# Two more pairs transposed by DMA instead of TensorE, and four output stores held back

## The chip, the cores and the metric

The kernel runs on one core of a Trainium2 chip. The metric is the device time of one execution in microseconds (us), given as the median over runs. Matmuls run on TensorE (PE), their weight loads are listed apart (PEld), and the other engines are VectorE (DVE), ScalarE (ACT), GpSimd (POOL) and SyncE (SP, which here only issues DMAs).

## The reference, cut to what matters

A chunked linear recurrence (4 batches, 8 heads, 768 positions, head size 32, state size 16) gives `x`, 3072 tokens by 256; a gated layer follows:

```python
L = exp(cum[i] - cum[j]) * (i >= j)                 # decay inside a chunk
y = ((C @ B.T) * L) @ x + (C @ state) * exp(cum)    # per batch, head, chunk
state = decay * state + (B * decay_from_j).T @ x
...
gate = maximum(x @ w_gate, 0)                       # 256 -> 1536
out = (gate * (x @ w_val)) @ w_out                  # 1536 -> 256
```

## The kernel before

**Tiling.** The 3072 tokens are cut into 12 pairs of 256 tokens (two chunks of 128) for the recurrence, and into 6 blocks of 512 tokens (two pairs) for the gated layer. While block `b` runs through the layer, the recurrence of the pairs of the next block is threaded between its matmuls: `P = 2b+2` and `Q = 2b+3`, and `W = 2b+1` is finished late. In block 1 these are pairs 4 and 5 (and W = 3), in block 2 pairs 6 and 7 (and W = 5).

**Order.** The order of the instructions on each engine is the order in the program text; `in_order` pins it. So an instruction that waits holds up all that stand behind it on its engine. Loads, stores and DMA transposes share SP's queue in the same way.

**The layer.** For each of 12 slices `f` of the 1536 columns, `gv` (or `gvh` in two halves) makes gate and val on PE, relu on ACT, and the product `h` on DVE; `fout` multiplies `h` by `w_out`; `foevac` copies the result to a buffer `ob` (three buffers that rotate) and stores it through SP.

**The recurrence of a pair.** B and C are loaded raw (`bcr`), and x (`xr`). POOL multiplies B and C by decay factors (`scale...`) and casts x to `xb` (`to_x`). B and C must then be transposed:

- Pairs 0 to 5: POOL writes `bs`; `turn` transposes it on PE (four 128x128 transposes in a pair, `transp`, L393), `bevac` copies B's result to `BT` on ACT, and `cevac` makes two masked copies `CT` of C's.
- Pairs 6 to 11 (`p >= NDMA`): `scale_padded` writes a zero-padded buffer `bz` (three of them, `turned`), with the two masked copies of C already in place, and one DMA transpose (L310) gives `TT`, read by PE directly.

`G` makes C times B transposed (L456; `G_rows`, L495, for pairs 6 on), `gevac` masks it on ACT, DVE and POOL (POOL's part is the affine selects, L171), `Dm` multiplies it with x (L634 and L687), `inter` adds the state's part (L623), `states` and `states_two` make the states (L573, L702), and `yevac` casts the result to `yT`, which the gates of the next block read.

**The stretch of the change.** In block 1 `turn(4)` and `turn(5)` stand among the gates at f = 6 and f = 8. `states(4)` stands at the beginning of the block, `inter(4)` at the end of the gates, `G(4)` and `G(5)` in the output matmuls. `states_two((6, 7))` stands near the beginning of block 2. In blocks 2 to 4 `Dm_two` stands behind eight of the twelve matmuls of the last output tile, and the last four cover the `yT` copies.

Of the kernel before, what the change touches and what calls it, by code (L numbers as in the profile page):

```python
# [8 lines left out]
FP32 = mybir.dt.float32  # L9
# [20 lines left out]
def kernel(  # L30
# [13 lines left out]
    nc = tc.nc  # L44
# [29 lines left out]
    def place(p):  # L74
        b, c0 = p // PPB, 2 * (p % PPB)
        return b, c0, slice(c0 * 128, (c0 + 2) * 128)
# [25 lines left out]
    def load(p, q):  # L102
        if "bcr" not in st.setdefault(p, {}):
            new_bc(p)
        load_bc(p, 1, q)
        load_bc(p, 0, q)
        new_x(p)
        for i in range(2):
            load_x(p, i, q)
# [183 lines left out]
    def scale_padded(p, eng, part=None):  # L293

        b, c0, _ = place(p)
        z = turned[p % 3]
        if part != 1:
            f = fac[:, b, c0:c0 + 2].rearrange("s i j h -> s i (j h)")
            eng.tensor_tensor(  # L299
                out=z.rearrange("s (i k) (h n) -> s i (k h) n", k=4, n=N)[:, :, 0:2 * NH],  # L300
                in0=st[p]["bcr"].rearrange("s i j h n -> s i (j h) n"),
                in1=f.to_broadcast([128, 2, 2 * NH, N]), op=ALU.mult)
            st[p]["B"] = [z[:, 4 * i] for i in range(2)]
        if part == 0:
            return
        parts = z.rearrange("s (i k) (q t n) -> s i k t q n", k=4, q=4, t=2)
        for t in range(2):
            eng.tensor_copy(out=parts[:, :, 2 + t, t], in_=parts[:, :, 1, t])
        tt = st[p]["TT"] = att.tile([128, 8, 128], BF16, tag="TT", name="TT", bufs=4)
        nc.sync.dma_start_transpose(out=tt, in_=z.rearrange("s k n -> s (k n)"))  # L310

    def new_bs(p):
        st[p]["bs"] = att.tile([128, 4, 128], BF16, tag="bs", name="bs", bufs=6)
# [38 lines left out]
    def scale_one(p, eng, j):  # L352

        b, c0, _ = place(p)
        for i in range(2):
            f = fac[:, b, c0 + i, j].rearrange("s (t q) -> s t q", t=2)
            eng.tensor_tensor(
                out=st[p]["bs"][:, 2 * i + j].rearrange("s (q t n) -> s t q n", q=4, t=2),
                in0=st[p]["bcr"][:, i, j].rearrange("s (t q) n -> s t q n", t=2),
                in1=f.to_broadcast([128, 2, 4, N]), op=ALU.mult)  # L360
# [60 lines left out]
    def ct(p, i, rows=slice(0, 128), t=None):  # L421
        if p < NWIDE:
            c = st[p]["CT"][rows, :, :, 64 * i:64 * i + 64]
        else:
            c = st[p]["CT"][rows, :, i]
        return c if t is None else c[:, t]

    def split(p, ap):

        return ap.rearrange("s t (r m) -> s t r m", r=2) if p < NWIDE else ap  # L430
# [17 lines left out]
    def G(p):  # L448
        s = st[p]
        if "gp" not in s:  # L450
            G_banks(p)
        g = s["gp"]
        for i in range(2):
            for q in range(4):
                r = slice(32 * q, 32 * q + 32)
                nc.tensor.matmul(  # L456
                    out=split(p, g[q][:, i]), lhsT=s["BT"][r, i], rhs=ct(p, i, r),
                    start=(i == 0), stop=True, tile_position=(32 * q, 0),
                    skip_group_check=True)
        s["gs"] = att.tile([128, 4, 4, 128], BF16, tag="gs", name="gs", bufs=2)  # L460
# [336 lines left out]
    def fout_last(b):  # L797

        r0 = b * 512 + 384
        for m in range(2):  # L800
# [6 lines left out]
            (nc.vector.tensor_copy if m else nc.scalar.copy)(out=ob, in_=o)  # L807
            (nc.sync if m else nc.scalar).dma_start(out=out[r0:r0 + 128, ms], in_=ob)

    def foevac(b, ts, o=None):  # L810
        last = b == NBLK - 1 and ts == 2
        if ts % 2 == 0 and not last:
            return
        ob = ffn.tile([128, 2, DM], FP32, tag="ob", name="ob", bufs=3)
        r0 = b * 512 + ts * 128
        if last:
            nc.scalar.copy(out=ob[:, 0], in_=fst["o"][:, 0])
            nc.scalar.dma_start(out=out[r0:r0 + 128, :], in_=ob[:, 0])
            return
        nc.scalar.copy(out=ob, in_=o or fst["o"])  # L820
        rows = out[r0 - 128:r0 + 128, :].rearrange("(i p) m -> p i m", p=128)
        for part in ((slice(0, 1), slice(1, 2)) if b in (2, 3) and ts == 3 else (slice(0, 2),)):
            nc.sync.dma_start(out=rows[:, part], in_=ob[:, part])


    B_, C_ = slice(0, 1), slice(1, 2)
# [91 lines left out]
    def turn(p):  # L918
        transp(p, 1)
        transp(p, 0)  # L920

    def tevac(p, beng, *cengs):
        bevac(p, beng)
        cevac(p, *cengs)
# [49 lines left out]
    for b in range(NBLK):  # L974
        P, Q, W = 2 * b + 2, 2 * b + 3, 2 * b + 1
        more = P < NPAIR
        if b == 1:
            load(P + 2, nc.sync)
            load(P + 3, nc.sync)
        if b == 2:  # L980
            scale(Q, nc.gpsimd)
            load(Q + 2, nc.sync)

        nh = (4, 6, 8, 0)[min(b, 3)]
        for f in range(nh):
            if b == 0:
                continue
            turning = f == (3 if b == 1 else nh - 3)
            gvh_mm(b, f, 0)
            gvh_relu(b, f, 0)  # L990
            gvh_mul(b, f, 0)
            if b == 1 and f == 1:
                to_x(P, nc.scalar)
            if turning:
                inter(W, 0)
                inter(W, 1)
                Dm(W)
                if b == 1:
                    states(P)
                    scale_one(P, nc.gpsimd, 1)  # L1000
                else:
                    states_two((P, Q))
                yevac(W, nc.scalar)
                if b == 1:
                    spread(P)
                else:
                    sums_two((P, Q))
# [4 lines left out]
        for f in range(nh, NF):  # L1012
            gv(b, f, b > 2 and f == 0)
            if b == 0:
                if f == 5:
                    over_sum(de_ps)
                if f == 7:
                    sevac(1, 1)
                if f == 9:
                    turn(P)  # L1020
                    tevac(P, nc.scalar, nc.vector)
                if f == 10:
                    held(Q, bc=False)
                if f == 11:
                    back(P)
                    backevac(P, nc.scalar)
            elif b == 1:
                if f == nh:
                    turn(P)
                    tevac(P, nc.scalar, nc.vector)  # L1030
                    scale(Q, nc.gpsimd)
                if f == 8:
                    turn(Q)
                    tevac(Q, nc.scalar, nc.vector)
                    scale(Q + 1, nc.gpsimd)
                    load(Q + 3, nc.sync)
            elif b == 2:
                if f == 9:
                    load(Q + 3, nc.sync)
            elif b == 3:  # L1040
                if f in (2, 6):
                    scale(P + 2 + f // 4, nc.gpsimd)
        if b == 1:
            inter(P, 0)
            inter(P, 1)
        if b == 0:

            for third in range(3):
# [16 lines left out]
                if third == 1:  # L1065
# [11 lines left out]
            A_ps[0] = rest  # L1077
            Dm(P)
            states(Q)
            held(Q + 2)  # L1080
            fout(b, 3, range(4))
            inter(P, 0)
            inter(P, 1)
            gevac(Q, after={2: lambda: [yevac_half(P, t, nc.scalar) for t in range(2)],
                            3: lambda: spread(Q)})
            new_bs(Q + 1)
            scale_one(Q + 1, nc.gpsimd, 0)
            fout(b, 3, range(4, NF))
            foevac(b, 3)
            continue  # L1090
        elif b == 1:
            fout(b, 0)
            G(P)
            gevac(P)
            over_sum2(de)
            fout(b, 1)
            foevac(b, 1)
            fout(b, 2)
        elif more:
            ahead = (P + 2, Q + 2) if Q + 2 < NPAIR else ()  # L1100
            fout(b, 0, range(9), True)
            G_rows(P)
            opened = y_banks()
            inter_rows(P, opened)
            inter_rows(Q, opened)
            gevac(P)
            if b == 2:
                scale_padded(Q + 2, nc.gpsimd, 0)
            fout(b, 0, range(9, NF))
            fout(b, 1)  # L1110
            first_two = fst["o"]
            fout(b, 2, range(1))
            G_rows(Q)
            gevac(Q)
            if b == 2:
                scale_padded(Q + 2, nc.gpsimd, 1)
                load(Q + 4, nc.sync)
                to_x(Q + 2, nc.scalar)
            foevac(b, 1, first_two)
            fout(b, 2, range(1, NF))  # L1120
            fout(b, 3, range(8))
            Dm_two((P, Q))
            states_two(ahead)
            yevac_two((P, Q))
            sums_two(ahead)
            fout(b, 3, range(8, NF))
            foevac(b, 3)
            continue
        else:
            fout(b, 0)  # L1130
            fout(b, 1)
            foevac(b, 1)
            fout(b, 2)
            foevac(b, 2)
            fout_last(b)
            continue
# [40 lines left out]
```

## Time and profile before

| | |
|---|---|
| median of 3 runs | 121.92 us (121.68 to 122.03) |
| profiled execution | 121.89 us, its span 120.2 us, so 1.69 us lie around the span |
| busy share of the span | PE 97%, DVE 73%, ACT 65%, POOL 42% |
| granted TensorE clock | full in every slice |
| DMA moved | 13.70 MB |

The span is cut by the profile in 40 slices of 3 us. A group of matmuls in the chain of waits is shown with the time from its start to that of the next piece, so its pieces add up to the span; the groups' mean of one matmul is its whole duration, which overlaps that of its neighbours.

### The profile page before, as it was taken

The page shows a single profiled execution, that of the slowest core. Times are in us where ns is not written, and L with a number is a line of the kernel's source. Part 1 is how long each engine was busy: PE and PEld are TensorE (multiplying, and loading weights), DVE is VectorE, ACT ScalarE, POOL GpSimd, SP SyncE. Part 2 cuts the span into 40 slices and gives each one's busy share as a digit, 9 for nine tenths or more (in the row PEclk, how much of TensorE's full clock was granted, in tenths as well). Part 3 has the DMA queues.
Part 4 walks back from the last instruction along what each step waited for, and adds up shares of the span by engine and source line. Part 5 has one row for each costly group of instructions (what it writes and reads, how often), then busy time and mean ns, then how long its engine had stood idle before and what let it go on. Part 6 is the DMA issues. An engine that isn't in the chain of part 4 may idle for free.

```text
span 120.2 us, 3322 instructions
## 1 busy us (share of the span) xinstructions
PE 116.1 (97%) x1237; PEld 75.0 (62%) x1237; DVE 87.6 (73%) x206; ACT 77.7 (65%) x170; POOL 50.4 (42%) x102
## 2 busy tenths in 40 slices
PE   7999999999999999999999999999999999999990
PEld 2446754677885577887577544578444677444790
DVE  6896779976899866899775787856787775678500
ACT  4288977687998726888626776535767445767240
POOL 6788999744406271956047542433400033000000
PEclk9999999999999999999999999999999999999999
DMA  3999999999969999799999699922200002200022
GB/s 67 213 187 176 206 185 196 205 128 124 160 69 193 125 100 138 100 172 169 118 171 104 94 145 147 266 68 87 87 0 5 0 0 93 87 0 0 0 87 87
DMA packets 80595, 13.70 MB, mean 114 GB/s; under 512 B 73420, under 2 KB 80580, under 8 KB 80580
## 3 DMA queue, kind: packets, MB, share of 16 engines
q1 hardware_dynamic: 73092, 10.55, 56.3%
q0 software_dynamic: 4080, 2.36, 14.2%
q10 hardware_dynamic: 3408, 0.59, 2.6%
q8 instruction: 9, 0.15, 0.5%
q14 instruction: 6, 0.05, 0.1%
HBM read 11.13 MB, written 3.15 MB: 119 GB/s over the span
## 4 chain that ended last, share of the span: by engine, by line
PE 95%; ACT 1%; DVE 0%; issue 0%
PE o L792 26%; PE gate L747 19%; PE val L747 19%; PE gv L762 14%; PE w L200 4%; PE g L495 2%; PE g L456 2%; PE y L687 1%; PE y L634 1%; PE o L804 1%; PE tp L393 1%; PE A_ps L237 1%; PE y L623 1%; ACT CT L417 1%; PE bt L437 1%; PE y L674 0%
## 5 line engine op out<-in xcount | busy, mean ns | idle before, releaser
L751 DVE TENSOR_TENSOR h<-r,val 128x512 bf16<-128x512 bf16 x54 | 36.9, 687 | 9.1 <-ACT r L750 6.6
L750 ACT ACTIVATE r<-gate 128x512 bf16<-128x512 f32 x54 | 32.2, 597 | 11.9 <-PE gate L747 11.2
L792 PE MATMUL o<-wo,h 128*128 128x256 bf16 x276 | 33.8, 273 | 0.0
L747 PE MATMUL val<-yT,wv 128*128 128x512 bf16 x108 | 32.6, 379 | 0.0
L747 PE MATMUL gate<-yT,wg 128*128 128x512 bf16 x108 | 32.6, 379 | 0.0
L792 PEld LDWEIGHTS <-h 128*128 128x128 bf16 x276 | 25.7, 98 | 5.4 <-issue 1.2
L171 POOL TENSOR_SCALAR_AFFINE_SELECT gs<-gs 128x512 bf16<-128x512 bf16 (+1 forms) x24 | 12.1, 528 | 27.8 <-ACT gs L468 27.8
L479 DVE TENSOR_TENSOR gs<-g,masks 128x512 bf16<-128x512 f32 x24 | 15.4, 685 | 6.0 <-PE g L495 2.8
L747 PEld LDWEIGHTS <-wv 128*128 128x128 bf16 x108 | 10.6, 98 | 12.5
L747 PEld LDWEIGHTS <-wg 128*128 128x128 bf16 x108 | 10.4, 98 | 11.1
L772 DVE TENSOR_TENSOR h<-r,gv 128x256 bf16<-128x256 bf16 x36 | 14.2, 417 | 1.3 <-ACT r L769 1.1
L769 ACT ACTIVATE r<-gv 128x256 bf16<-128x256 f32 x36 | 13.7, 389 | 1.2
L468 ACT CAST gs<-g 128x512 bf16<-128x512 f32 x12 | 7.0, 586 | 11.2 <-PE g L495 5.8
L762 PE MATMUL gv<-yT,wg 128*128 128x256 bf16 x72 | 13.9, 273 | 0.2
L762 PE MATMUL gv<-yT,wv 128*128 128x256 bf16 x72 | 13.9, 273 | 0.0
L299 POOL TENSOR_TENSOR bz<-bcr,fac 128x512 bf16<-128x512 f32 x6 | 6.4, 1059 | 7.1 <-DMA bcr<-in_B_dram 7.1
L820 ACT COPY ob<-o 128x512 f32<-128x512 f32 x11 | 6.5, 591 | 4.2 <-PE o L792 4.1
L322 ACT CAST yT<-y 128x256 bf16<-128x256 f32 (+1 forms) x11 | 5.4, 516 | 4.7 <-PE y L687 2.8
L762 PEld LDWEIGHTS <-wv 128*128 128x128 bf16 x72 | 7.0, 98 | 1.1 <-issue 0.3
L762 PEld LDWEIGHTS <-wg 128*128 128x128 bf16 x72 | 6.8, 98 | 1.0 <-issue 0.2
L200 PE MATMUL w<-const-bfloat16-1.0 128*128 128x512 bf16 (+3 forms) x15 | 5.7, 498 | 0.8 <-PEq L1161 0.8
L322 POOL CAST xb<-xr 128x512 bf16<-128x512 f32 (+1 forms) x8 | 4.7, 591 | 3.2 <-DMA xr<-in_x_dram 3.1
(118 smaller groups left out, 110.8 us busy)
## 6 DMA issues: line engine op xcount, KB each, us to landing
xr<-in_x_dram SPq DMA_DIRECT2D x24, 128.0 KB, 3.2
out_dram<-ob SPq DMA_DIRECT2D x9, 256.0 KB, 2.4
bcr<-in_B_dram SPq DMA_DIRECT2D x16, 64.0 KB, 2.9
bcr<-in_C_dram SPq DMA_DIRECT2D x16, 64.0 KB, 2.9
wg<-in_moe_w_gate_dram POOLq DMA_DIRECT2D x6, 128.0 KB, 4.4
wv<-in_moe_w_val_dram POOLq DMA_DIRECT2D x6, 128.0 KB, 4.9
wo<-in_moe_w_out_dram POOLq DMA_DIRECT2D x3, 256.0 KB, 7.2
out_dram<-ob SPq DMA_DIRECT2D x4, 128.0 KB, 2.5
```

The lines of the kernel that those rows point to most:

```text
L171: nc.gpsimd.affine_select(out=dst, in_=dst, pattern=pattern, compare_op=ALU.is_ge, fill=0.0, base=0, channel_multiplier=-1)
L200: nc.tensor.matmul(out=w[:, 0:cols], lhsT=nc.const_aps.tensor(1.0, [128, 128], BF16), rhs=nc.const_aps.tensor(1.0, [128, cols], BF16), sta ...
L322: (eng.copy if eng is nc.scalar else eng.tensor_copy)(out=out, in_=in_)
L468: nc.scalar.copy(out=d[:, 0], in_=g[0])
L479: nc.vector.tensor_tensor(out=d[:, q], in0=g[q], in1=m, op=ALU.mult)
L747: nc.tensor.matmul(out=o, lhsT=w_tile(ws, f, k), rhs=yT[:, k, tk], start=(k == 0), stop=(k == 1), skip_group_check=True)
L750: nc.scalar.activation(r, g, AF.Relu)
L751: nc.vector.tensor_tensor(out=fst[b][:, f], in0=r, in1=v, op=ALU.mult)
L762: nc.tensor.matmul(out=gv_[:, j], lhsT=w_tile((wgs, wvs)[j], f, k), rhs=yT[:, k, tk], start=(k == 0 and not (early and j)), stop=(k == 1), ...
L769: nc.scalar.activation(r[:, 0:256], fst[b, f, u][:, 0], AF.Relu)
L772: nc.vector.tensor_tensor(out=fst[b][:, f, u * 256:(u + 1) * 256], in0=fst.pop((b, f, u, "r"))[:, 0:256], in1=fst.pop((b, f, u))[:, 1], op ...
L792: nc.tensor.matmul(out=o[:, ts % 2], lhsT=fst[b][:, f, ts * 128:(ts + 1) * 128], rhs=wo[:, f], start=(f == 0 and new), stop=(f == NF - 1), ...
```

## The change

Pairs 4 and 5 go the way of the DMA transposes. A new `scale_turned` writes B and the two masked copies of C into the padded buffer in four POOL instructions per pair; `turn_padded` is the DMA transpose. `G`, `inter` and `states` of these pairs read `TT` and `bz`. `turn`, `bevac` and `cevac` of the two pairs go (eight PE transposes, two ACT copies, four DVE copies). The transposes of pairs 4 and 5, and the loads around them, stand in a new order on SP. `to_x(5)` moves to the beginning of block 1, `to_x(6)` behind `gevac(4)`. The four stores of blocks 0 and 1 get four buffers of their own and are issued behind the gates of block 3; the last stores of blocks 2 and 3 are no longer split in two. In block 4 `Dm_two` stands one output matmul earlier (behind seven).

```diff
+        turn_padded(p)
+
+    def scale_turned(p, eng):
+        b, c0, _ = place(p)
+        z = turned[p % 3]
+        dst = z.rearrange("s (i k) (q t n) -> s i k t q n", k=4, q=4, t=2)
+        src = st[p]["bcr"].rearrange("s i j (t q) n -> s i j t q n", t=2)
+        f = fac[:, b, c0:c0 + 2]
+        for j in range(2):
+            for t in range(2):
+                eng.tensor_tensor(
+                    out=dst[:, :, j * (2 + t), t], in0=src[:, :, j, t],
+                    in1=f[:, :, j, 4 * t:4 * t + 4].to_broadcast([128, 2, 4, N]), op=ALU.mult)
+        st[p]["B"] = [z[:, 4 * i] for i in range(2)]
+
+    def turn_padded(p):
         tt = st[p]["TT"] = att.tile([128, 8, 128], BF16, tag="TT", name="TT", bufs=4)
-        nc.sync.dma_start_transpose(out=tt, in_=z.rearrange("s k n -> s (k n)"))
+        nc.sync.dma_start_transpose(out=tt, in_=turned[p % 3].rearrange("s k n -> s (k n)"))
...
-            c = st[p]["CT"][rows, :, i]
+            c = st[p]["TT"][rows, 4 * i + 2:4 * i + 4]
...
-                    out=split(p, g[q][:, i]), lhsT=s["BT"][r, i], rhs=ct(p, i, r),
+                    out=split(p, g[q][:, i]), rhs=ct(p, i, r),
+                    lhsT=s["BT"][r, i] if p < NWIDE else s["TT"][r, 4 * i],
...
-        ob = ffn.tile([128, 2, DM], FP32, tag="ob", name="ob", bufs=3)
+        early = b < 2
+        ob = ffn.tile([128, 2, DM], FP32, tag="obe" if early else "ob", name="ob",
+                      bufs=4 if early else 3)
...
-        for part in ((slice(0, 1), slice(1, 2)) if b in (2, 3) and ts == 3 else (slice(0, 2),)):
-            nc.sync.dma_start(out=rows[:, part], in_=ob[:, part])
+        if early:
+            late_store.append((rows, ob))
+        else:
+            nc.sync.dma_start(out=rows, in_=ob)
...
         if b == 1:
-            load(P + 2, nc.sync)
+            new_bc(P + 2)
+            load_bc(P + 2, 1, nc.sync)
+            load_bc(P + 2, 0, nc.sync)
+            scale_turned(Q, nc.gpsimd)
+            turn_padded(Q)
+            new_x(P + 2)
+            for i in range(2):
+                load_x(P + 2, i, nc.sync)
             load(P + 3, nc.sync)
+            to_x(Q, nc.gpsimd)
...
                     states(P)
-                    scale_one(P, nc.gpsimd, 1)
...
             elif b == 1:
-                if f == nh:
-                    turn(P)
-                    tevac(P, nc.scalar, nc.vector)
-                    scale(Q, nc.gpsimd)
                 if f == 8:
-                    turn(Q)
-                    tevac(Q, nc.scalar, nc.vector)
-                    scale(Q + 1, nc.gpsimd)
+                    scale_padded(Q + 1, nc.gpsimd)
                     load(Q + 3, nc.sync)
...
+        if b == 3:
+            for rows, ob in late_store:
+                nc.sync.dma_start(out=rows, in_=ob)
...
-            held(Q + 2)
+            held(Q + 2, with_x=False)
...
-            new_bs(Q + 1)
-            scale_one(Q + 1, nc.gpsimd, 0)
+            scale_turned(Q + 1, nc.gpsimd)
+            turn_padded(Q + 1)
+            new_x(Q + 2)
+            for i in range(2):
+                load_x(Q + 2, i, nc.sync)
...
             gevac(P)
+            to_x(P + 2, nc.gpsimd)
             over_sum2(de)
...
-            fout(b, 3, range(8))
+            early = 8 if ahead else 7
+            fout(b, 3, range(early))
...
-            fout(b, 3, range(8, NF))
+            fout(b, 3, range(early, NF))
```

More of the change, by code (lines that the diff above doesn't have):

```diff
@@ L808, in fout_last @@
             (nc.sync if m else nc.scalar).dma_start(out=out[r0:r0 + 128, ms], in_=ob)
+    late_store = []
     def foevac(b, ts, o=None):
```

## The prediction

> **What bounds the kernel now.** I read the page's busy shares first, then its chain by engine, then the stretches around block 1.
>
> ```profile
> PE 116.1 (97%) x1237; PEld 75.0 (62%) x1237; DVE 87.6 (73%) x206; ACT 77.7 (65%) x170; POOL 50.4 (42%) x102
> DMA  3999999999969999799999699922200002200022
> ...
> PE 95%; ACT 1%; DVE 0%; issue 0%
> ```
>
> PE is busy for 97% of the span and carries 95% of the chain that ended last. So time comes off only where PE gets less to do or loses a wait, and time is added only where PE must wait. The DMA engines are nine tenths busy or more in most of the first 26 slices (3 us each, so to 78 us), and much less after that. The chain in order of time shows the stretch of the change (start, length, what).
>
> ```profile
> 36.61 0.43 PE val L747 x2
> 37.04 0.22 PE tp L393 x4
> 37.26 0.43 PE gate L747 x2
> ...
> 38.99 0.22 PE tp L393 x4
> ...
> 41.80 0.22 PE y L623 x4
> ...
> 46.76 0.33 PE g L456 x8
> ...
> 51.68 0.12 PE A_ps L702 x16
> ```
>
> Each piece starts where the last one ends: 36.61 + 0.43 = 37.04, + 0.22 = 37.26. There is no gap in which PE waits, so a step taken out here shortens the chain by its own piece. One microsecond of the same stretch by engine (PE, PEld, DVE, ACT, POOL, clock, DMA share, GB/s) agrees: PE 1.00 at full clock.
>
> ```profile
> 38.00:39.00 1.00, 1.00 (x9) 0.53 (x8) 1.00 (x3) 0.73 (x2) 0.57 (x1) 1.00 1.10 116
> L393 PE MATMUL tp<-ident,bs 128*128 128x128 bf16 x20 | 2.2, 227 | 0.0
> ```
>
> **Part 1: eight PE transposes go.** The chain gives 0.22 us for four, so 2 x 0.22 = 0.44 us come off. The group's mean of 227 ns is one transpose from its beginning to its end; in the chain one starts every 0.22 / 4 = 55 ns, because they overlap, and 55 ns is what I take. The Trainium skill's page "TensorE: Matmul & The Clock Gate", section "Part 4: PE-mode transpose", gives about 275 ns for one 128x128 transpose inside a kernel; by that figure eight would be an estimate of 2.2 us and the sum 119.6 us. The trace shows 227 ns as the duration, near that figure, and 55 ns as the step, and the step decides.
>
> The two ACT copies to BT and the four DVE copies to CT that go with the transposes lie beside PE, which has no gap there; I cost them at nothing. The G and inter matmuls keep their number and shape with other operands: 0.33 and 0.22 us stay.
>
> **Part 2: what PE will wait for instead.** Pair 4's `TT` must have landed for `inter(4)`, at 41.80 - 0.44 = 41.36, pair 5's for `G(5)` at 46.76 - 0.44 = 46.32, pair 4's scaled B for `states(4)`, which now starts at 32.31. POOL first, then SP:
>
> ```profile
> 32.31 0.26 PE L573 MATMUL A_ps<-xb,bs 128*32 128x64 bf16 x12
> 29.88 0.76 POOL L357 TENSOR_TENSOR bs<-bcr,fac 128x128 bf16<-128x128 f32 x2
> 31.56 0.40 POOL L357 TENSOR_TENSOR bs<-bcr,fac 128x128 bf16<-128x128 f32 x1 [0.22 <-DMA bcr<-in_C_dram]
> 36.13 1.20 POOL L348 TENSOR_TENSOR bs<-bcr,fac 128x256 bf16<-128x256 f32 x2 [4.17 <-DMA bcr<-in_B_dram]
> 48.89 1.06 POOL L299 TENSOR_TENSOR bz<-bcr,fac 128x512 bf16<-128x512 f32 x1
> 50.48 0.61 POOL L322 CAST xb<-xr 128x512 bf16<-128x512 f32 x1
> ```
>
> ```profile
> 28.12 1.41 SPq L92 DMA_DIRECT2D bcr<-in_C_dram x2
> 29.62 0.57 SPq L823 DMA_DIRECT2D out_dram<-ob x1
> 31.52 2.67 SPq L92 DMA_DIRECT2D bcr<-in_B_dram x2
> 35.54 0.82 SPq L823 DMA_DIRECT2D out_dram<-ob x1
> 39.23 1.20 SPq L100 DMA_DIRECT2D xr<-in_x_dram x2
> 43.72 1.23 SPq L100 DMA_DIRECT2D xr<-in_x_dram x2
> 45.05 2.88 SPq L310 DMA_TRANSPOSE TT<-bz x1
> L310 SPq DMA_TRANSPOSE TT<-bz x6: 1251/1299/2882, 45.0 to 76.6; - x6
> DMA to landing us min/median/max: 2.7/3.2/5.5
> ```
>
> `states(4)`: the B part of `scale_turned(4)` is again two instructions of 0.40 us; before they ran from 29.88 to 30.64, and nothing ahead of them changes. 1.7 us of room.
>
> Pair 4's transpose: its C part is two more instructions of 0.40 us, from 31.56 on (the last C has landed), so to 32.36. On SP the transpose stands behind pair 5's B, whose issue ended at 31.52 + 2.67 = 34.19; without the store ahead of it that is 0.57 earlier, 33.6, and later than POOL. So: issue 33.6, landing 3.2 after the issue's start at the median, 36.8; at the longest, 5.5, 39.1. Needed at 41.36: 2.3 to 4.6 us of room.
>
> Pair 5's transpose: POOL began pair 5's scaling at 36.13, when its B had landed; now some 0.57 sooner, 35.6, and four instructions of 0.40 end at 37.2. On SP it stands where pair 6's x began, 39.23; both stores are gone (-0.57 - 0.82) and pair 4's transpose is ahead (+1.30): 39.1. Landing 42.3, at the longest 44.6; needed at 46.32: 1.7 to 4.0 us of room.
>
> What is queued behind: everything up to pair 7's x, which ended its issue at 43.72 + 1.23 = 44.95. Now -0.57 - 0.82 + 2 x 1.30 = +1.21, so 46.16. Of two like issues the second starts 0.6 sooner, 45.5.
>
> ```profile
> xr<-in_x_dram SPq DMA_DIRECT2D x24, 128.0 KB, 3.2
> ```
>
> It lands at 45.5 + 3.2 = 48.7. POOL cast pair 7's x at 50.48, now at 50.04 (it hangs on `G(5)` through the affine selects, which come 0.44 sooner); PE wants it in `states_two` at 51.68 - 0.44 = 51.24, and the cast takes 0.61, so PE waits only if it lands after 51.24 - 0.61 = 50.63. Room 1.9 us. Pair 7's B, loaded just before, is needed at 48.45 by the scaling on POOL, with the same slack to PE behind it. I cost the two added DMA transposes and their waits at nothing on PE; the bounds are zero and the case of the second rival, below. Below nothing they cannot go, as PE has no wait here that earlier loads could remove.
>
> `to_x(6)` now stands behind the affine selects of `G(4)`, where POOL next waits for `G(5)`; `to_x(5)` stands ahead of block 1's gates and its reader, `states(5)`, behind them. Both nothing.
>
> **Part 3: the stores.** Two 256 KB stores of block 0 and two of block 1 leave the busy stretch. They come back behind the last transposes:
>
> ```profile
> 75.18 2.65 SPq L310 DMA_TRANSPOSE TT<-bz x2
> 82.36 33.39 SPq L823 DMA_DIRECT2D out_dram<-ob x6
> ```
>
> SP is free from 77.83 to 82.36, 4.5 us; four issues at the 0.82 us above are 3.3 us, and the DMA row above has at most two tenths from there on. Nobody reads these buffers again, and the three other buffers wait only for stores a block older. Nothing on PE, nothing at the end of the kernel, 35 us later.
>
> **Part 4: block 4's `Dm_two` one matmul earlier.**
>
> ```profile
> 100.95 0.58 ACT L322 CAST yT<-y 128x512 bf16<-128x512 f32 x1 [1.12 <-PE y L687]
> 101.12 0.54 PE o L792 x4
> 101.66 0.30 PE gate L747
> 101.96 0.22 PE val L747
> ```
>
> The first gate of block 5 takes 0.30 where the next matmul of that size takes 0.22: its `yT` is cast until 101.53, and 0.08 us of waiting is left. With five output matmuls as cover instead of four (0.54 / 4 or 5: 0.11 us more) it goes. -0.08 us; the other end is nothing.
>
> **Sum.** Profiled execution 121.89 - 0.44 - 0.08 = 121.37 us. That execution lies 0.03 below the median of 121.92, so 121.40 us. The runs before spread from 121.68 to 122.03; about 0.3% (0.37 us) is what a measurement can tell from no change, so "same" is 121.55 to 122.29, and my forecast is 0.15 us beyond it.
>
> **Rivals.** *PE gains less than its pieces.* PE has slack that the chain hides, or a wait of 0.15 to 0.5 us takes the place of the transposes: 121.6 to 122.0 us. For it: PEld is busy only 0.53 in the window row. Against it: the pieces follow each other at 0.43 us per two matmuls whatever PEld does. The Trainium skill's page "Perfetto Trace Analysis", section "Identifying the Most-Contended Engine", says that matmul busy share tells little of the distance to the roofline and that the share of LDWEIGHTS should be taken. By that rule PE at 62% would have room, and the cut would be worth about nothing; the gapless chain speaks against it here. Chance 0.16.
>
> *Pair 7 comes late (slower).* The transposes are slow to issue in the full stretch: if both take 2.88 us as the one at 45.05 did, pair 7's x is issued 2 x 1.58 = 3.2 us later, at 48.7, lands at 51.9, is cast at 52.5, and PE, wanting it at 51.24, waits 1.3 us: 121.40 + 1.3 = 122.7; with a landing 2.3 us longer (5.5 instead of 3.2) 125.0. It decides from a landing after 50.63 on, and makes the kernel slower than the bound from 51.5 on. For it: DMA at nine tenths, and the first transpose of before, the one in this stretch, was the slow one. Against: 1.9 us of room. Chance 0.16.
>
> *A transpose costs PE its whole duration*: 8 x 0.227 = 1.8, 120.1 us. The chain speaks against it. Chance 0.02.
>
> **How the numbers follow.** The forecast, 121.40, has what is left, 0.66, and its own range is 121.2 to 121.6. Faster: 0.66 + 0.02 = 0.68; same 0.16; slower 0.16. The range goes down to 121.1 (spread of the runs) and up to 122.3, the beginning of the slow rival; that leaves out the whole-duration case and most of the slow one, some 0.17.
>
> **What would show it.** In the profile after: no L393 rows between 30 and 50 us; the pieces val and gate of block 1 meeting directly; `inter(4)` at 41.4 and `G(5)` at 46.3; pair 4's transpose issued near 33.6 and pair 5's near 39.1; `states_two` at 51.2 with POOL's cast ended before; the first gate of block 5 at 0.22; four stores issued between 78 and 82. A PE piece of more than its usual length at `inter(4)`, `G(5)` or `states_two`, with a DMA or POOL as releaser, would make it wrong.

## The result: 0.4% faster, and the profile after

| | before | after |
|---|---|---|
| median of 22 runs each, same chip | 122.01 us (121.61 to 124.06) | 121.53 us (121.11 to 125.51) |
| ratio, undisturbed runs | | 0.9962, 95% interval 0.9946 to 0.9979 |
| profiled execution | 121.89 us, span 120.2 | 121.42 us, span 119.7 |

The profiled execution is 0.47 us shorter, the runs by 0.38%, some 0.46 us; forecast were 0.52 us. The ratio leaves out executions over 1.5% longer than the fastest of the same kernel. Its interval lies wholly below 1, but not wholly below 0.997, the 0.3% that the prediction took as its bound: a gain is shown, a gain of over 0.3% is only likely.

The chain of waits after, in order of time (start, length, what; L765 are gate and val, L641 `inter`, L473 `G`, L720 `states_two`):

```profile
36.46 0.59 PE val L765 x2
37.05 0.43 PE gate L765 x2
37.48 0.43 PE val L765 x2
...
38.78 0.43 PE gate L765 x2
...
41.37 0.22 PE y L641 x4
...
46.33 0.33 PE g L473 x8
...
51.25 0.12 PE A_ps L720 x16
...
100.58 0.65 PE o L810 x5
101.23 0.22 PE gate L765
...
116.90 0.29 DVE ob L825
```

The val matmuls meet the next gates directly (37.05, 38.78); the transposes are gone. `inter(4)` stands at 41.37, `G(5)` at 46.33, `states_two` at 51.25, each within 0.01 us of the place forecast, so PE waits at none. The first gate of block 5 takes 0.22 instead of 0.30.

SP's queue after (start, length, engine, line, what; L327 is the DMA transpose, L1070 the stores held back):

```profile
30.78 1.33 SPq L92 DMA_DIRECT2D bcr<-in_B_dram  x2
32.22 2.46 SPq L327 DMA_TRANSPOSE TT<-bz  x1
...
39.07 1.25 SPq L327 DMA_TRANSPOSE TT<-bz  x1
...
44.71 1.15 SPq L100 DMA_DIRECT2D xr<-in_x_dram  x2
45.96 2.96 SPq L327 DMA_TRANSPOSE TT<-bz  x1
...
73.39 2.70 SPq L327 DMA_TRANSPOSE TT<-bz  x2
76.14 2.17 SPq L1070 DMA_DIRECT2D out_dram<-ob  x4
81.93 0.37 SPq L847 DMA_DIRECT2D out_dram<-ob  x1
```

Pair 5's transpose is issued at 39.07, pair 7's x until 45.86, and the four stores take 2.17 us of a free stretch. POOL casts pair 7's x without waiting, and the cast ends 0.6 us before PE wants it:

```profile
50.05 0.61 POOL L339 CAST xb<-xr 128x512 bf16<-128x512 f32 x1
```

But that x took longer to land than the 3.2 us of the sum. The two loads of pair 7's x, first before, then after:

```profile
L100 SPq DMA_DIRECT2D xr<-in_x_dram x2: 581/592/602, 43.7 to 44.3; - x2
DMA to landing us min/median/max: 4.4/4.5/4.6
```

```profile
L100 SPq DMA_DIRECT2D xr<-in_x_dram x2: 527/554/581, 44.7 to 45.3; - x2
DMA to landing us min/median/max: 4.3/4.4/4.4
```

The second load after started at 45.3 and landed 4.3 us later, at 49.6, where 48.7 was forecast. PE would wait from a landing after 50.63 on, so 1.0 us of room was left here, not 1.9.

**A measure free of the beginning.** The loads of the first 30 us arrive differently from run to run: block 1's first gate began between 36.09 and 38.39 us in the traces read below, though the kernels are alike for the first 28 us, where most of this arises. So the runs below are read by a stretch as well, from block 1's first gate to the last copy on DVE (the L825 row above; L807 before): 36.17 to 117.41 before, 81.24 us; 36.19 to 116.90 after, 80.71 us, or 0.53 less.

### The profile page after: what moved, and what is told of

Same layout as the page of the kernel before. It is cut to its first block, busy times and chain, and to the rows that moved or that the text cites. A ratio compares the mean times of both kernels' runs of the same rounds, so it can differ in the third digit from the quotient of the medians.

```text
span 119.7 us, 3291 instructions
## 1 busy us (share of the span) xinstructions
PE 115.0 (96%) x1222; PEld 74.6 (62%) x1229; DVE 87.1 (73%) x202; ACT 77.0 (64%) x168; POOL 51.2 (43%) x104
## 3 DMA queue, kind: packets, MB, share of 16 engines
q0 software_dynamic: 4080, 2.36, 14.0%
## 4 chain that ended last, share of the span: by engine, by line
PE 95%; ACT 1%; issue 0%; DVE 0%
PE o L810 26%; PE gate L765 19%; PE val L765 19%; PE gv L780 14%; PE w L200 4%; PE g L513 2%; PE g L473 2%; PE y L705 1%; PE y L652 1%; PE o L822 1%; PE A_ps L237 1%; PE tp L410 1%; PE y L641 1%; ACT CT L434 1%; PE bt L454 1%; PE y L692 0%
## 5 line engine op out<-in xcount | busy, mean ns | idle before, releaser
L765 PE MATMUL gate<-yT,wg 128*128 128x512 bf16 x105 | 32.0, 379 | 0.2
L765 PE MATMUL val<-yT,wv 128*128 128x512 bf16 x105 | 31.5, 379 | 0.2
L765 PEld LDWEIGHTS <-wv 128*128 128x128 bf16 x108 | 10.6, 98 | 12.4
L765 PEld LDWEIGHTS <-wg 128*128 128x128 bf16 x108 | 10.5, 98 | 11.5
L200 PE MATMUL w<-const-bfloat16-1.0 128*128 128x512 bf16 (+3 forms) x14 | 5.2, 498 | 0.8 <-PEq L1194 0.8
```

Source lines behind the costliest of these rows:

```text
L200: nc.tensor.matmul(out=w[:, 0:cols], lhsT=nc.const_aps.tensor(1.0, [128, 128], BF16), rhs=nc.const_aps.tensor(1.0, [128, cols], BF16), sta ...
L765: nc.tensor.matmul(out=o, lhsT=w_tile(ws, f, k), rhs=yT[:, k, tk], start=(k == 0), stop=(k == 1), skip_group_check=True)
```

## The experiments

My theory: PE has no gap, so the gain is the eight transposes (0.44 us) and the wait that the moved `Dm_two` hides (0.08 us), and the stores and DMA transposes are hidden. Rivals: the relief of ACT and DVE; the stores themselves; a queue so full that the hiding fails.

**1. The transposes put back on PE**, nothing else:

```diff
+    def pe_turns(n):
+        tp = mm.tile([128, 2, 2, 128], BF16, tag="tp", name="tpd")
+        for k in range(n):
+            nc.tensor.transpose(out=tp[:, (k // 2) % 2, k % 2], in_=ident, identity=ident)
...
             elif b == 1:
+                if f in (nh, 8):
+                    pe_turns(4)     # 16 in the second run
```

> The changed kernel with eight transposes of the identity put back on TensorE at f = 6 and f = 8 of block 1; nothing reads them, so the ACT and DVE copies stay away and the DMA transposes stay. My theory (PE's steps are the gain): 0.44 us more than the changed kernel, 0.9993 of the time before. Rival 1 (the copies that went from ACT and DVE are the gain): no more than the changed kernel, 0.996. Rival 2 (a transpose costs its whole 227 ns): 1.8 us more than the changed kernel, 1.011.

> The same with 32 transposes of the identity instead of eight (16 at each place), to measure one. My theory, 55 ns each: 1.76 us more than the changed kernel, 123.3 us, 1.011 of the time before. Rival, 227 ns each: 7.3 us more, 128.8 us. Rival, PE has room: no more than the changed kernel.

Measured: 1.0021 of before (0.9981 to 1.006) with eight, too wide to tell; 1.0107 (1.0081 to 1.0132), 123.51 us, with 32. The chains, first with eight, then with 32:

```profile
37.47 0.22 PE tpd L831 x4
...
39.42 0.22 PE tpd L831 x4
...
52.11 0.25 PE A_ps L720 x16
```

```profile
37.02 0.89 PE tpd L831 x16
...
39.64 0.89 PE tpd L831 x16
```

Four cost 0.22 us and sixteen 0.89, 56 ns each. The stretch with 32 is 36.16 to 118.65, 82.49 us, which is 1.78 more than after: 2 x 0.89 to the hundredth. With eight it is 36.61 to 117.90, 81.29, or 0.58 more: 0.44 and another 0.13 at `states_two` (0.25 instead of 0.12), where pair 7's x came late in that execution and POOL's cast waited for it:

```profile
51.46 0.61 POOL L339 CAST xb<-xr 128x512 bf16<-128x512 f32 x1 [0.36 <-DMA xr<-in_x_dram]
```

The cast ended at 52.07, just ahead of PE at 52.11. Had the added transposes not put PE back by 0.44 us, it would have waited some 0.4 us, by an estimate from these rows, so in this execution the room was used up.

The runs tell the price of a transpose, and that the price comes back in full with ACT's and DVE's copies still away. Relief of those engines isn't the gain, and 227 ns isn't the price.

**2. Each part alone.** The transposes alone, with the stores and `Dm_two` in their places of before (the last stores of blocks 2 and 3 stay in one piece):

```diff
-        early = b < 2
+        early = False
...
-            early = 8 if ahead else 7
+            early = 8
```

> Pairs 4 and 5 go by DMA transposes, but the four stores stay in their old places and block 4's Dm_two stays behind eight output matmuls. My theory (the gain is the eight PE transposes, 0.44 us, and the moved Dm_two, 0.08): 0.44 us less than before, 121.5 to 121.6, L393's eight pieces gone and the first gate of block 5 again at 0.30. The two stores of block 0 add 1.4 us to SP's queue ahead of pair 7's x, so its issue goes from 45.3 to 46.7 and the landing to about 50.2, still ahead of the 50.6 from which PE waits. Rival (the stores had to be moved, since the queue is full): PE waits in states_two or at G(5), 0.3 us or more, and the time is that of before or longer, 121.9 to 123.

Measured: 124.03 us, 1.0168 of before (1.0131 to 1.0206). The rival is right, by more than it said. The stretch is 36.83 to 119.12, 82.29 us; without waits it should be 80.71 + 0.08 = 80.79, so PE waits 1.50 us. The timeline of PE and the chain further on:

```profile
52.46 0.24 PE L720 MATMUL A_ps<-xb,bz 128*32 128x64 bf16 x8 [0.51 <-POOL xb L339]
...
63.05 3.43 DMA xr<-in_x_dram
...
66.56 0.62 ACT xb L339
67.17 0.49 ACT ob L842
...
67.71 0.27 PE A_ps L720 x12
```

PE waits 0.51 us in `states_two` for pair 7's cast, and once more in the next `states_two`, for pair 9: its x lands at 66.48, ACT casts it until 67.18, and a copy of `ob` stands behind that in the chain. SP's queue shows why pair 7 came late:

```profile
46.77 2.33 SPq L100 DMA_DIRECT2D xr<-in_x_dram  x2
49.20 1.74 SPq L327 DMA_TRANSPOSE TT<-bz  x1
```

Pair 7's x is issued until 49.10, 3.2 us later than in the changed kernel; 0.64 of that is the later beginning of block 1 in this execution, the two stores of block 0 are 0.55 and 0.64, and one of the two x issues took over a microsecond longer than the other.

The other parts alone, on the kernel before (the change's lines on `late_store`, `obe` and `early`, pairs 4 and 5 on TensorE), were run twice:

> The kernel before with only the stores held back and block 4's Dm_two one matmul earlier; pairs 4 and 5 stay on TensorE. My theory: only the 0.08 us of the first gate of block 5, so 0.9993 of the time before, not told apart from it by timing; in the trace the chain is that of before up to block 4. Rival (the stores were what held the kernel up): 0.3 us or more less, 0.997 or below.

Measured: 122.49 us, 1.003 (0.9998 to 1.0062), which timing can't tell from no change. The profiled execution took 126.09 us at a granted clock of 0.986, with the first gate of block 1 only at 40.30, so its trace settles nothing.

> The kernel before with only the stores held back and block 4's Dm_two one matmul earlier, a second time, for a clean trace. Theory: the stretch from block 1's first gate to the last copy is 0.08 us shorter than in the kernel before, 81.16 us, the first gate of block 5 at 0.22 instead of 0.30, and the time within 0.2% of that before. Rival (holding the stores back costs or gains something by itself): a stretch that differs from 81.16 by more than 0.1.

Measured: 121.99 us, 0.9963 (0.9908 to 1.0017), again no difference that timing can tell. Its trace has the full clock throughout: 36.17 to 117.32, 81.15 us, 0.09 less than before, with the first gate of block 5 at its usual length:

```profile
36.17 0.22 PE gate L747
...
101.66 0.22 PE gate L747
...
117.32 0.29 DVE ob L807
```

So stores held back gain nothing by themselves; with the DMA transposes they keep away 1.5 us of waits, as far as these two traces go.

**3. How much room is left.** DMA transposes of a weight tile into spare buffers, which nobody reads, ahead of pair 7's loads:

```diff
+            for k in range(1):     # 2 in the second run
+                spare = glob.tile([128, 8, 128], BF16, name="spare%d" % k)
+                nc.sync.dma_start_transpose(
+                    out=spare, in_=wo[:, 0:4].rearrange("p f m -> p (f m)"))
             load(P + 3, nc.sync)
```

> The changed kernel with one more 256 KB DMA transpose on SP (of a weight tile into a spare buffer that nobody reads), ahead of pair 7's loads. It measures how much later pair 7's x may come before PE waits in states_two. In the changed kernel's trace the second of its two issues starts at 45.3 and PE would wait for a landing after 50.6. One more transpose is 1.3 us on SP, so 46.6 and a landing of 49.7 at the median of 3.1. My theory as predicted (1.9 us of room): no wait, the stretch from block 1's first gate to the last copy stays at 80.7 us. Rival, after the run with the stores in their old places, where 1.4 us of stores already made PE wait 0.5 us: a wait of 0.1 to 0.6 us in states_two, 80.8 to 81.3.

> The same with two more DMA transposes ahead of pair 7's loads: 2.6 us on SP, landing at 51.0 by the median and up to 53 in a full queue. My theory as predicted: a wait of 0.4 us or so in states_two, 81.1 us for the stretch. Rival (the room is used up already): 1.5 us or more, and later pairs come late as well, 82.3 us or more.

Measured: 122.71 us, 1.0075 (1.0051 to 1.0099), with one; 125.62 us, 1.0295 (1.0254 to 1.0336), with two. PE's timeline, first of the run with one, then with two:

```profile
52.01 0.24 PE L720 MATMUL A_ps<-xb,bz 128*32 128x64 bf16 x8 [0.64 <-POOL xb L339]
```

```profile
53.22 0.24 PE L720 MATMUL A_ps<-xb,bz 128*32 128x64 bf16 x8 [1.86 <-POOL xb L339]
```

The second transpose adds 1.86 - 0.64 = 1.22 us, about its issue time on SP: the room is used up by the first, as the rival had it. The stretch with one is 36.25 to 117.78, 81.53 us, 0.82 more than after and a little more than the rival said. With two, neither the time nor the stretch measures the transposes alone, as both executions had a lower granted clock (0.986 and 0.982). In the profiled one the 40 matmuls behind `states_two` took 6.14 us at a clock of 0.72, where after they took 4.47:

```profile
53.46 6.14 PE gv L780 x40
```

Where the room goes, with one (chain, then SP):

```profile
48.26 2.96 DMA xr<-in_x_dram
51.22 0.02 issue
...
51.34 0.62 POOL xb L339
```

```profile
39.72 1.36 SPq L327 DMA_TRANSPOSE TT<-bz  x1
...
42.42 1.59 SPq L1012 DMA_TRANSPOSE spare<-wo  x1
...
47.08 1.76 SPq L100 DMA_DIRECT2D xr<-in_x_dram  x2
```

The landing at 51.22 is 0.59 behind the forecast limit of 50.63, and the wait is 0.64: the limit was right, and here the landing took 2.96 us, near the 3.2 of the sum. But the second x issue of pair 7 starts at 48.26, 3.0 us later than the 45.3 of the changed kernel's trace, where the added transpose took 1.59. The rest is SP itself: 0.65 behind already at pair 5's transpose (39.72 against 39.07), 0.6 in the x issues (1.76 against 1.15). And x wasn't alone. POOL began to scale pair 7's B at 49.48, where after it began at 48.46, since that B came late too:

```profile
49.48 1.06 POOL L299 TENSOR_TENSOR bz<-bcr,fac 128x512 bf16<-128x512 f32 x1 [0.94 <-PE gv L780]
```

(The row names PE as releaser; B landed at 49.23.) From this scaling to the cast of x POOL needs 1.59 us, as after (48.46 to 50.05), so by an estimate from these rows B alone would have made PE wait 0.4 us or so.

**4. Which stores.**

```diff
-        early = b < 2
+        early = b < 1     # block 1's stores back; in the second run b == 1: block 0's back
```

> The changed kernel with only block 0's two stores held back; block 1's two stores are again issued where block 1 ends, ahead of pair 7's transpose and pair 9's loads. With all four in place PE waited in states_two for pair 7 and again for pair 9. My theory now (each pair of stores takes SP's time from the pairs behind it): no wait for pair 7, the wait for pair 9 stays, 0.3 to 0.9 us, so the stretch is 81.0 to 81.6 us and the time 121.8 to 122.4. Rival (one late pair makes the next one late, so block 0's stores alone are the cause): no wait at all, 80.7 us, 121.5.

Measured: 121.69 us, 0.998 (0.9951 to 1.001). The stretch is 36.17 to 116.93, 80.76 us, and no PE row between 30 and 90 us shows a wait. My theory fell here and the rival holds: block 1's stores could have stayed. So pair 9's wait in experiment 2 needed block 0's stores too. Whether it came through the wait at pair 7 or through the fuller queue isn't told apart: with block 0's stores alone, below, PE waits at pair 7 and not at pair 9.

> The counterpart of the run with block 1's stores put back: here only block 1's two stores are held back, and block 0's two go out where block 0 ends, ahead of the loads of pairs 5 and 6. My theory now (block 0's stores alone cost the room that the two transposes need): PE waits in states_two for pair 7's x, 0.3 to 0.8 us, as with all four in place; with block 1's stores away, pair 9 is less late than there, so the stretch from block 1's first gate to the last copy lies between 81.0 and 82.0 us, against 80.7 in the changed kernel and 82.3 with all four in place. Rival (it takes all four): no wait, 80.7 us.

Measured: 123.61 us, 1.0063 (0.9984 to 1.0143), which timing can't tell from no change. The first gate came only at 38.39, 2.2 us later than after, but SP ran later still: pair 7's x was issued from 48.42 instead of 44.71, 3.7 us later. PE waits for pair 7 (chain, then PE):

```profile
47.66 3.53 DMA bcr<-in_B_dram
...
51.44 1.07 POOL bz L299
...
53.70 0.24 PE L720 MATMUL A_ps<-xb,bz 128*32 128x64 bf16 x8 [0.21 <-POOL xb L339]
...
119.47 0.29 DVE ob L825
```

The stretch is 81.08 us, 0.37 more than after, inside the forecast. The wait, 0.21, is less than the 0.3 that I gave as the least, and it comes by pair 7's B, which landed at 51.19 and was scaled from 51.44 on, not by its x. Much of its longer time lies ahead of block 1 and isn't explained by the stores.

**5. The changed kernel again**, beside the runs with one and two more transposes and with block 1's stores back:

> The changed kernel itself, for a comparison on the same chip as the other runs. Theory: the stretch from block 1's first gate to the last copy is 80.7 us again, 0.53 less than in the kernel before; ratio of the times 0.996. Rival (the first measurement was lucky in the loads of the first 30 us): 0.998 to 1.0 with the stretch longer than 80.9.

Measured: 121.67 us against 121.98, 0.9976 (0.9951 to 1.0002); the stretch is 36.09 to 116.80, 80.71 us, the same to the hundredth, so by the stretch the rival fell. The trace shows how thin the cover is (SP; pair 7's second B load; POOL):

```profile
45.48 2.39 SPq L100 DMA_DIRECT2D xr<-in_x_dram  x2
```

```profile
L92 SPq DMA_DIRECT2D bcr<-in_B_dram x1: 581/581/581, 44.8 to 44.8; - x1
DMA to landing us min/median/max: 3.7/3.7/3.7
```

```profile
48.73 1.06 POOL L299 TENSOR_TENSOR bz<-bcr,fac 128x512 bf16<-128x512 f32 x1 [0.34 <-PE gv L780]
```

The same two x issues end at 47.87 instead of 45.86. But it is B that sets the cast: it landed at 44.8 + 3.7 = 48.5, POOL scaled it from 48.73 on and cast x from 50.32 to 50.93, against PE's need at some 51.15. So 0.2 us were left.

## Why the prediction was right, point by point

- **Part 1, eight transposes.** 0.44 us by the chain's step of 55 ns; shown by the runs with eight (0.22 for four) and 32 (56 ns each). The Trainium skill's page "TensorE: Matmul & The Clock Gate", "Part 4: PE-mode transpose", gives some 275 ns for one, a duration; 275 x 32 would have been 8.8 us, and the stretch grew by 1.78.
- **Part 2, the places.** `inter(4)`, `G(5)` and `states_two` at 41.37, 46.33 and 51.25 against 41.36, 46.32 and 51.24; pair 5's transpose at 39.07 against 39.1; pair 7's x issued until 45.86 against 46.16. Pair 4's transpose went out at 32.22 instead of 33.6, as the loads ahead of it took 1.33 us instead of 2.67, but its own issue took 2.46 instead of 1.30: the end, 34.68 against 34.9, came out by luck.
- **Part 2, the room of 1.9 us: mis-sized.** POOL's side held: the limit of 50.63, and the cast at 50.05 against 50.04. Three things did not. The landing: I took 3.2 us, the median of all 24 x loads, but pair 7's own took 4.3 to 4.4, and 4.4 to 4.6 already in the kernel before, where I could have read it. Pair 7's B: I gave it a limit (scaling from 48.45 on, with the slack behind it) and never said when it lands; in the second trace of the changed kernel it came last, with 0.2 us left. SP: I took the issue times of one execution as fixed and shifted them, but the same two issues took 1.15 to 2.39 us, and pair 5's transpose started between 39.07 and 39.82. So 1.0 us of room was left in one trace of the changed kernel, 0.2 in the other and none in that of the run with eight, and one more transpose, 1.3 us by my price, made PE wait 0.64 us. That PE waited for nothing was right, but by less than I said and in part by luck.
- **Part 3, the stores.** At the end of the kernel they cost nothing, as said: 2.17 us of a free 4.5. But counting their leaving at nothing was right only against the kernel before. The sum of part 2 had them in it (-0.57 - 0.82), and the prediction didn't say what the change would be without: 1.9 - 1.4 = 0.5 us of room by its numbers, so still no wait; measured, 1.50 us of waits in the trace and a kernel 1.7% slower than before.
- **Part 4, `Dm_two`.** 0.08 forecast, 0.09 measured with that part and the stores alone; 0.30 became 0.22.
- **The rivals.** "Pair 7 comes late" is real, and holding back block 0's two stores is what kept it out. "PE has slack" fell with experiment 1: the 1.78 us put in came out whole at the end. The Trainium skill's page "Perfetto Trace Analysis", "Identifying the Most-Contended Engine", would judge PE's headroom by MFU (the share of peak FLOPs) and the share of LDWEIGHTS, the latter 62% here; for whether a cut in PE's work shortens this kernel, the gapless chain told more.

## What to carry to other kernels

Where the chain is one engine without a gap, price its work by the step from one piece to the next, not by an instruction's duration, and the sum comes out to a few hundredths. When work is moved to a queue, the room of whoever is last in it decides. Read that room from the landing of the very transfer that comes last, not from the median of its kind, and for every input that its reader needs. Take it from several executions, or probe it with one dummy transfer, before calling the move free.

## What was unexpected on the hardware

- The issue of one DMA on SP varies between two executions of the same kernel: pair 7's two x loads took 1.15 and 2.39 us, pair 6's transpose behind them 2.96 and 1.25 us.
- The long issue falls at much the same time and hits whatever stands there. In both traces a packet of the profile's instruction queue (q8; packets, MB, share) begins then, between 46.9 and 47.2 us in the first and between 45.9 and 46.3 in the repeat:

```profile
q8 instruction: 1, 0.02, 18.3%
```

```profile
q8 instruction: 1, 0.02, 22.0%
```

  Near 33 us it is the same: a packet begins between 32.9 and 33.2 in both, and pair 4's transpose takes 2.46 and 2.36 us. Whether that packet holds SP up, no run here shows.
- In a full queue what is added passes on: 1.2 to 1.6 us more on SP ahead of pair 7 made PE wait there and, with the four stores in place, for pair 9 again 15 us later (52.46 and 67.71).
- Sixteen transposes of 128x128 in a row step at 56 ns, though one lasts 219 ns there (227 in the kernel before).
